# Batch 3's q and v loads and v casts moved, and batch 1's feature maps one slot earlier, in a fused attention and FFN kernel

## Chip, cores, metric

One NeuronCore of one Trainium2 chip. The metric is the time of one execution on the device in microseconds (us). The kernel was run several times; the profile is of one execution. Engines: PE is TensorE, DVE is VectorE, ACT is ScalarE, POOL is GpSimd, SP issues DMAs.

## The reference, cut to what matters

```python
def phi(x, c, s):                       # c, s: cos, sin of pi/2 * position / 576
    r = np.maximum(x, 0.0)
    return np.concatenate([r * c, r * s], axis=-1)
q_p, k_p = phi(q, cos_w, sin_w), phi(k, cos_w, sin_w)      # q, k, v: 8 batches, 8 heads, 576 x 64
kv  = np.einsum('bhsf,bhsd->bhfd', k_p, v)
z   = np.sum(k_p, axis=2)
num = np.einsum('bhsf,bhfd->bhsd', q_p, kv)
den = np.einsum('bhsf,bhf->bhs', q_p, z)[..., None] + 1e-06
# x = num / den, heads side by side: 4608 tokens x 512; then
xn  = x / np.sqrt(np.mean(x * x, axis=-1, keepdims=True) + 1e-06) * rms_g
g, val = xn @ w_gate, xn @ w_val        # 512 -> 1536
out = (silu(g) * val) @ w_out           # 1536 -> 512
```

## The kernel before

The program is scheduled by hand. Block b is the FFN of batch b (block 8 takes the last 64 tokens of every batch). A block has 16 slots: slots 0 to 11 make one 128-wide piece of gate and value each (8 matmuls on PE, 1.73 us, then `sg` = silu on ACT and the product `hT` on DVE), slots 12 to 15 make one output tile each (12 matmuls, 2.6 us). The attention of batch b+1 is strewn into block b: the helper `at(block, slot, where, f, ...)` puts a call before the slot's matmuls ("pe"), before its silu and product ("pre") or behind them ("post"). In the traces PE and DVE take their own lists in order (figures under step 3 below), so a slot number decides behind what an instruction stands. phi is the feature map of the reference, made of q and k in two halves (the cosine half on DVE, the sine half on ACT); `xnT` is x, normalised and transposed, which the FFN reads; the k-v product (`kv` and `z` of the reference) needs phi of k and v in bf16.

```python
# block 0: phi of k of batch 1, and q tile 0
for j in range(NJ):                                   # NJ = 9
    at(0, 7 + j // 2, "post", k_phi, V, 1, j, 0)      # cosine half on DVE
    at(0, 7 + j // 2, "post", k_phi, A, 1, j, 1)      # sine half on ACT
at(0, 11, "post", q_phi, V, 1, 0, 0)
at(0, 11, "post", q_phi, A, 1, 0, 1)
# ... (cut)
for nb in range(2, B):                                # batch nb is prepared in block b
    b = nb - 1
    late = nb == 2
    vb, vn = (b, 3) if late else (b - 1, 14)
    # ... phi of k at slots 12 to 14 of block b - 1 (cut)
    for c in range(5):                                # phi and DMA transpose of q, tile c
        qn = (2, 3, 5, 5, 6)[c] if late else c + 2 * (nb == 3)
        at(b, qn, "post", q_phi, V, nb, c, 0)
        at(b, qn, "post", q_phi, A, nb, c, 1)
        at(b, qn, "post", q_tr_dma, nb, c)
    if not late:
        at(vb, vn, "post", v_cast, V, nb, *LOW)       # v to bf16 on DVE, two halves
    at(vb, vn + 1, "post", v_cast, V, nb, *HIGH)
    kz, nds = (6, (7, 9, 11, 12)) if late else (4, (6, 8, 10, 12) if nb == 3 else (5, 7, 9, 11))
    at(b, kz, "pe", kvz_pe, nb, psA)                  # k-v product: 72 small matmuls, LOW then HIGH
    # ... its copies, the numerators nd at slots nds, x_norm and the xnT transpose a slot later (cut)
for nb in range(3, B):                                # loads, on SP
    b = nb - 2
    for i, which in enumerate(("k", "v", "q")):
        for p in range(5 if which == "q" else 4):     # 4 pieces of 256 or 288 KB; q also a tail
            n = (0, 6, 9)[i] + p if b == 1 else 5 * i + p
            at(b + n // 16, n % 16, "post", load_piece, which, nb, p)
# ... between blocks 0 and 1: output of block 0, attention of batch 1
for n in range(NNT - 2):
    if 1 <= n <= 4:
        q_tr_pe(1, n - 1, qbank[n - 1])               # PE transposes q of batch 1
    # ... (cut)
```

`raw` tiles of q and v exist once, so a load has to wait until the previous batch's phi or cast has read it. Block b+1 starts with matmuls on `xnT`, whose last quarter is a DMA transpose issued at slot 13 of block b.

Of the kernel before, what the change touches and what calls it, by code (L numbers as in the profile page):

```python
# [23 lines left out]
def kernel(  # L24
# [39 lines left out]
    V, A, G = nc.vector, nc.scalar, nc.gpsimd  # L64
    NJ = 9
    LOW, HIGH = (0, 2), (2, 4)
# [565 lines left out]
    def none():  # L632
        return {"pe": [], "mid": [], "pre": [], "post": []}
# [3 lines left out]
    def at(blk, n, where, f, *args):  # L637
        slots.setdefault((blk, n), none())[where].append((f, args))
# [17 lines left out]


    for j in range(NJ):
        at(0, 7 + j // 2, "post", k_phi, V, 1, j, 0)
        at(0, 7 + j // 2, "post", k_phi, A, 1, j, 1)  # L660
    at(0, 11, "post", q_phi, V, 1, 0, 0)
    at(0, 11, "post", q_phi, A, 1, 0, 1)


    for nb in range(2, B):
        b = nb - 1
        late = nb == 2
        vb, vn = (b, 3) if late else (b - 1, 14)
        if late:
            at(vb, vn, "post", v_cast, V, nb, *LOW)  # L670
        for j in range(NJ):
            kb, kn = (b, 1 + j // 7) if late else (b - 1, 12 + j // 3)
            if not late or j > 3:
                at(kb, kn, "post", k_phi, V, nb, j, 0)
            if not late or j > 1:
                at(kb, kn, "post", k_phi, A, nb, j, 1)
        for c in range(5):
            qn = (2, 3, 5, 5, 6)[c] if late else c + 2 * (nb == 3)
            at(b, qn, "post", q_phi, V, nb, c, 0)
            at(b, qn, "post", q_phi, A, nb, c, 1)  # L680
            at(b, qn, "post", q_tr_dma, nb, c)
        if not late:
            at(vb, vn, "post", v_cast, V, nb, *LOW)
        at(vb, vn + 1, "post", v_cast, V, nb, *HIGH)
        kz, nds = (6, (7, 9, 11, 12)) if late else (4, (6, 8, 10, 12) if nb == 3 else (5, 7, 9, 11))
        at(b, kz, "pe", kvz_pe, nb, psA)
        at(b, kz, "pre", kvz_evac, A, nb, psA, 0)
        at(b, kz, "pre", kvz_evac, A, nb, psA, 1)
        for j in range(4):
            n = nds[j]  # L690
            at(b, n, "mid" if n == NNT else "pe", nd_pe, nb, j, psA)
            at(b, n, "pre", nd_post, nb, j, psA)
            at(b, n, "post", x_sq, nb, j)
            where = "pre" if n + 1 >= NNT else "post"
            at(b, n + 1, where, x_norm, nb, j)
            at(b, n + 1, where, x_tr_dma, nb, j)
        if nb % 2 == 1:
            at(b, 13, "pe", nd_pe, nb, 4, psA)
            at(b, 13, "pre", nd_post, nb, 4, psA)
            at(b, 13, "post", x_sq, nb, 4)  # L700
            at(b, 14, "post", x_norm, nb, 4)
            at(b, 14, "post", x_tr_dma, nb, 4)
    for nb in range(3, B):

        b = nb - 2
        for i, which in enumerate(("k", "v", "q")):
            for p in range(5 if which == "q" else 4):
                n = (0, 6, 9)[i] + p if b == 1 else 5 * i + p
                at(b + n // 16, n % 16, "post", load_piece, which, nb, p)

    def gval_step(blk, n, bank=None):
# [31 lines left out]
    for n in range(NNT - 2):  # L743
# [4 lines left out]
        if 1 <= n <= 4:  # L748
            c = n - 1
# [22 lines left out]
        if n in nd_at:  # L772
            j = nd_at[n]
# [94 lines left out]
```

## Time and profile before

| | before |
|---|---|
| runs at hand for the prediction | 328.82, 559.21, 328.21 us |
| span of the profiled execution | 327.5 us, granted TensorE clock 1.00 |
| PE busy | 317.4 us (97%) |
| DVE, ACT busy | 57%, 54% |

The first line of the page's table of engines (busy time, share of the span, number of instructions):

```profile
PE 317.4 (97%) x2441; PEld 160.6 (49%) x2441; DVE 186.1 (57%) x412; ACT 176.6 (54%) x366; POOL 32.0 (10%) x67
```

With PE at 97%, only PE's idle time can be won. The list of waits, PE alone (total us, times, longest):

```profile
PE psO L479 <- ACT kpm L209: 1.7, 1, 1.7
PE psO L466 <- DVE warm L145: 1.2, 1, 1.2
PE psV L254 <- DVE qp L211: 1.0, 1, 1.0
PE psG L426 <- DMA xnT<-xn: 0.7, 1, 0.7
PE psG L565 <- DVE xnT L265: 0.5, 1, 0.5
PE psO L254 <- ACT qp L209: 0.3, 1, 0.3
```

All but the third and fourth lie in the first 20 us, which the change leaves alone. The third is here in the timeline (start, duration, engine, line, operation; in brackets the idle time before it and what ended it):

```profile
40.14 0.59 PE L446 MATMUL psC<-wo,hT 128*128 128x512 bf16 x2
40.37 2.55 ACT L209 ACTIVATE qp<-rq,tab 128x512 bf16<-128x512 f32 x4
40.41 0.69 DVE L441 TENSOR_TENSOR hT<-psV,sg 128x512 bf16<-128x512 f32 x1 [0.51 <-PE psV L426]
41.02 0.34 DVE L211 TENSOR_SCALAR kpm<-rk,tab 128x256 bf16<-128x256 f32 x1
41.28 1.12 DVE L211 TENSOR_SCALAR qp<-rq,tab 128x512 bf16<-128x512 f32 x2
...
42.16 0.33 PE L254 MATMUL psV<-ident,qp 128*128 128x128 bf16 x3 [0.99 <-DVE qp L211]
```

DVE started the product of slot 11 at 40.41, the last phi of k at 41.02 and phi of q at 41.28, in the order of its list, and PE waited 0.99 us for that. The fourth, in the timeline of the end of block 1, with the k-v product of batch 3 some 7 us later:

```profile
85.59 0.42 SPq L90 DMA_DIRECT2D rq<-in_q_dram  x1
...
87.02 1.70 SPq L406 DMA_TRANSPOSE xnT<-xn  x1
...
92.41 1.02 PE L426 MATMUL psG<-xnT,wg 128*128 128x512 bf16 x4 [0.73 <-DMA xnT<-xn]
...
99.41 1.34 PE L282 MATMUL psA<-vvm,kpm 64*128 64x65 bf16 x72
```

A piece of q goes out 1.43 us ahead of the transpose. The view of the tile `xnT`, cut to that transpose, gives the time from its issue to its landing:

```profile
L406 SPq DMA_TRANSPOSE xnT<-xn x1: 1698/1698/1698, 87.0 to 87.0; - x1
...
DMA to landing us min/median/max: 5.3/5.3/5.3
```

The k-v product runs through in 1.34 us; its v was cast in block 1.

### The profile page before, as it was taken

To read this page: it belongs to the slowest core of one execution; us is meant where nothing else is said; L and a number is where in the kernel's file an instruction comes from. 1 tells how busy PE (TensorE), PEld (TensorE's weight loads), DVE (VectorE), ACT (ScalarE), POOL (GpSimd) and SP (SyncE) were. 2 spreads that over 40 slices of the span, in tenths; PEclk is the share of its full clock that TensorE was granted. 3 is DMA by queue.
4 is the path that set the end of the run, shared out by engine and by line. 5 is a ranking of instruction groups with operands and counts; after the bars stand their busy time and mean duration, and the time that the engine had idled before them with its cause. 6 is when DMAs were issued, how large, how long until landed. Compare 5 with 4: busy or idle time off the path is not lost.

```text
span 327.5 us, 6440 instructions
## 1 busy us (share of the span) xinstructions
PE 317.4 (97%) x2441; PEld 160.6 (49%) x2441; DVE 186.1 (57%) x412; ACT 176.6 (54%) x366; POOL 32.0 (10%) x67
## 2 busy tenths in 40 slices
PE   6999989999999999999999999999999999999994
PEld 2587455554435444544454445444544444444442
DVE  6875668787745876578257745773577133203310
ACT  6963865965656457645654576556644233223321
POOL 1660022001100110011001100110011000000000
PEclk9999999999999999999999999999999999999999
DMA  7999999899978966976597569967621400020014
GB/s 253 244 195 266 309 174 331 311 170 220 235 202 154 228 171 169 218 208 164 179 221 195 150 197 214 188 174 214 127 47 32 130 32 0 29 101 1 0 34 96
DMA packets 80337, 53.91 MB, mean 165 GB/s; under 512 B 51377, under 2 KB 67761, under 8 KB 80306
## 3 DMA queue, kind: packets, MB, share of 16 engines
q1 hardware_dynamic: 73264, 48.64, 58.6%
q0 software_dynamic: 6880, 4.72, 10.1%
q8 instruction: 19, 0.31, 0.4%
q14 instruction: 12, 0.10, 0.2%
q10 hardware_dynamic: 162, 0.13, 0.1%
HBM read 37.75 MB, written 9.44 MB: 144 GB/s over the span
## 4 chain that ended last, share of the span: by engine, by line
PE 84%; ACT 5%; DVE 4%; DMA 3%; issue 2%; POOL 0%; ACTq 0%; DVEq 0%
PE psG L426 25%; PE psV L426 24%; PE psC L446 23%; PE psA L282 3%; ACT kpm L209 2%; PE psA L310 2%; DMA xnT<-xn 2%; PE psG L446 1%; PE psG L565 1%; DMA rk<-in_k_dram 1%; PE psV L565 1%; DVE xt L364 1%; PE psO L565 1%; DVE xn L387 1%; ACT sg L435 1%
## 5 line engine op out<-in xcount | busy, mean ns | idle before, releaser
L441 DVE TENSOR_TENSOR hT<-psV,sg 128x512 bf16<-128x512 f32 x102 | 70.3, 690 | 97.7 <-PE psV L426 86.8
L435 ACT ACTIVATE sg<-psG 128x512 f32<-128x512 f32 x102 | 60.6, 594 | 67.0 <-PE psG L426 66.9
L426 PE MATMUL psG<-xnT,wg 128*128 128x512 bf16 (+1 forms) x368 | 92.9, 375 | 0.8 <-DMA xnT<-xn 0.7
L426 PE MATMUL psV<-xnT,wv 128*128 128x512 bf16 (+1 forms) x368 | 92.7, 374 | 0.0
L446 PE MATMUL psC<-wo,hT 128*128 128x512 bf16 x396 | 89.6, 379 | 0.0
L426 PEld LDWEIGHTS <-wv 128*128 128x128 bf16 x416 | 40.6, 98 | 47.4
L446 PEld LDWEIGHTS <-hT 128*128 128x128 bf16 x420 | 40.2, 98 | 46.4
L426 PEld LDWEIGHTS <-wg 128*128 128x128 bf16 x416 | 38.5, 98 | 42.2 <-issue 1.0
L263 ACT COPY osb<-psC 128x512 f32<-128x512 f32 (+1 forms) x33 | 19.2, 582 | 41.0 <-PE psC L446 39.6
L380 POOL TENSOR_TENSOR rs<-ms,mhalf 128x1 f32<-128x1 f32 x36 | 19.8, 550 | 200.6 <-ACT scr L375 200.6
L387 DVE SCALAR_TENSOR_TENSOR xn<-xt,rs,gb 128x512 bf16<-128x512 f32 x36 | 26.8, 746 | 14.7 <-POOL rs L380 14.7
L375 ACT ACTIVATE scr<-xt 128x513 bf16<-128x513 f32 x36 | 22.9, 635 | 21.5 <-DVE xt L364 21.2
L209 ACT ACTIVATE kpm<-rk,tab 128x256 bf16<-128x256 f32 (+1 forms) x78 | 32.0, 477 | 1.7 <-DMA rk<-in_k_dram 1.7
L364 DVE TENSOR_TENSOR xt<-psA,rec 128x512 f32<-128x512 f32 x35 | 24.2, 691 | 1.2
L211 DVE TENSOR_SCALAR kpm<-rk,tab 128x256 bf16<-128x256 f32 (+1 forms) x84 | 22.3, 330 | 2.2 <-DMA rk<-in_k_dram 2.2
L209 ACT ACTIVATE qp<-rq,tab 128x512 bf16<-128x512 f32 x32 | 22.4, 713 | 0.0
L211 DVE TENSOR_SCALAR qp<-rq,tab 128x512 bf16<-128x512 f32 x32 | 15.3, 494 | 0.0
L310 PEld LDWEIGHTS <-qpT 128*128 128x128 bf16 x248 | 11.6, 98 | 6.7 <-issue 0.2
L310 PE MATMUL psA<-kvzs,qpT 128*128 128x65 bf16 x248 | 12.8, 194 | 0.2
L426 PE MATMUL psV<-xnt_tail,wv 128*128 128x512 bf16 x48 | 12.3, 379 | 0.0
L426 PE MATMUL psG<-xnt_tail,wg 128*128 128x512 bf16 x48 | 12.3, 379 | 0.0
L282 PEld LDWEIGHTS <-kpm 64*128 64x128 bf16 x576 | 9.9, 95 | 3.6 <-issue 3.1
(89 smaller groups left out, 166.7 us busy)
## 6 DMA issues: line engine op xcount, KB each, us to landing
out_dram<-osb SPq DMA_DIRECT2D x32, 256.0 KB, 2.5
rv<-in_v_dram SPq DMA_DIRECT2D x21, 288.0 KB, 3.4
rk<-in_k_dram SPq DMA_DIRECT2D x20, 288.0 KB, 3.6
rq<-in_q_dram SPq DMA_DIRECT2D x20, 256.0 KB, 3.4
rk<-in_k_dram SPq DMA_DIRECT2D x2, 1152.0 KB, 8.7
rq<-in_q_dram SPq DMA_DIRECT2D x2, 1024.0 KB, 8.9
rv<-in_v_dram SPq DMA_DIRECT2D x3, 576.0 KB, 8.6
wo<-in_moe_w_out_dram POOLq DMA_DIRECT2D x4, 384.0 KB, 7.1
```

The costliest lines, as they stand in the source:

```text
L209: nc.scalar.activation(out=out_ap, in_=in_ap, func=AF.Relu, scale=scale)
L211: eng.tensor_scalar(out=out_ap, in0=in_ap, scalar1=scale, scalar2=0.0, op0=ALU.mult, op1=ALU.max)
L282: nc.tensor.matmul(banks[c][:, r * E : (r + 1) * E], lhsT=kp_main[b][lo : lo + 64, j, r, :], rhs=vvm[b % 2][lo : lo + 64, r, j, :], start= ...
L310: nc.tensor.matmul(o[:, g, i, :], lhsT=qpT[(b, 0)][:, h, j * P : (j + 1) * P], rhs=kvz_of(b, h), start=True, stop=True,)
L364: nc.vector.tensor_tensor(out=xt[:, 0:DM].rearrange("p (b h d) -> p b h d", b=2, d=D), in0=o[:, :, :, 0:D], in1=rec[:, :, :].unsqueeze(3). ...
L375: nc.scalar.activation(out=scr[:, :], in_=xt[:, 0 : DM + 1], func=AF.Square, scale=1.0 / math.sqrt(DM), accum_out=ms[:, :],)
L380: nc.gpsimd.tensor_tensor(out=rs[:, :], in0=ms[:, :], in1=mhalf[:, :], op=ALU.pow)
L387: nc.vector.scalar_tensor_tensor(out=xn[:, :], in0=x_of[(b, j)][:, 0:DM], scalar=rs_of[(b, j)][:, :], in1=gb[:, :], op0=ALU.mult, op1=ALU. ...
L426: nc.tensor.matmul(pst[bank][:, cols[0] : cols[1]], lhsT=w[:, t, n * P : (n + 1) * P], rhs=x[:, t, cols[0] : cols[1]], start=(t == 0), sto ...
L435: nc.scalar.activation(out=sg[:, :], in_=psG[bank][:, :], func=AF.Silu)
L441: nc.vector.tensor_tensor(out=hTs[blk][:, n, :], in0=psV[bank][:, :], in1=sg[:, :], op=ALU.mult)
L446: nc.tensor.matmul(bank, lhsT=hTs[blk][:, n, j * P : (j + 1) * P], rhs=wo[:, n, :], start=(n == 0), stop=(n == NNT - 1),)
```

## The change

The intent, in the words that came with it: q of batch 3 loaded at slots 6 to 10 and v at 13 to 16 of block 1, v cast in block 2, phi of q as in later batches; for batch 1 the cosine half of q tile 0 a slot sooner (the diff moves phi of k a slot sooner too).

```diff
     for j in range(NJ):
-        at(0, 7 + j // 2, "post", k_phi, V, 1, j, 0)
-        at(0, 7 + j // 2, "post", k_phi, A, 1, j, 1)
-    at(0, 11, "post", q_phi, V, 1, 0, 0)
+        at(0, 6 + j // 2, "post", k_phi, V, 1, j, 0)
+        at(0, 6 + j // 2, "post", k_phi, A, 1, j, 1)
+    at(0, 10, "post", q_phi, V, 1, 0, 0)
     at(0, 11, "post", q_phi, A, 1, 0, 1)
@@
         vb, vn = (b, 3) if late else (b - 1, 14)
+        if nb == 3:
+            vb, vn = b, 1
@@
-            qn = (2, 3, 5, 5, 6)[c] if late else c + 2 * (nb == 3)
+            qn = (2, 3, 5, 5, 6)[c] if late else c
@@
-        at(vb, vn + 1, "post", v_cast, V, nb, *HIGH)
-        kz, nds = (6, (7, 9, 11, 12)) if late else (4, (6, 8, 10, 12) if nb == 3 else (5, 7, 9, 11))
+        at(vb, vn + 1 + (nb == 3), "post", v_cast, V, nb, *HIGH)
+        kz, nds = (6, (7, 9, 11, 12)) if late else (4, (5, 7, 9, 11))
@@
-                n = (0, 6, 9)[i] + p if b == 1 else 5 * i + p
+                n = (0, 13, 6)[i] + p if b == 1 else 5 * i + p
```

## The prediction

> **What bounds the kernel.** TensorE: the engine table has it busy 317.4 of 327.5 us, at granted clock 1.00; DVE 57%, ACT 54%. The list of waits puts most of PE's 10 us of idle time into the first 20 us, untouched by the change. Later, two exceed 0.3 us:
> - 0.99 us at 41.17-42.16: PE's transposes of q of batch 1 wait for phi of q tile 0 (cosine half on DVE from 41.28, behind hT of slot 11).
> - 0.73 us at 91.68-92.41: block 2 waits for the last xnT transpose, issued at 87.02, landing after 5.35 us (shortest: 2.6), beside pieces of q and output stores.
>
> **What the change does.** No work is added or removed. By the instruction order:
> 1. Block 0: phi of k of batch 1 goes from slots 7-11 to 6-10, and the cosine half of q tile 0 goes ahead of hT of slot 11. Its k landed at about 31.0 (issued 20.97, 10.0 us); ACT gets there at 31.4. Its q landed at about 39.7 (32.03 plus 7.6); DVE gets there at 39.65. Both just in time: the halves are done by 40.7, before PE asks at 41.0. The 0.99 us go; v's casts then bind perhaps 0.15. Gain 0.85 us.
> 2. Block 1: q's pieces move to slots 6-10, before the last transposes; v's come at 13-16, behind them. [...] I expect 2.8 to 4 us; there is room for 4.66. Gain 0.7 us.
> 3. Block 2: both casts of v leave the end of block 1 and stand on DVE at slots 1 and 3. The second comes after hT and phi of q of slot 3, while PE wants it in the k-v product right behind slot 3's matmuls; that product now waits for DVE twice, before not at all. With block 2 starting at 0, PE is there at 6.9 and through the first half at 7.55. DVE starts hT of slot 3 at 7.17 (0.69 us), then phi (0.48), the cast (0.75): done at 9.0. PE waits about 1.45 us, and nothing gives it back. Batch 2's product shows such a wait already (0.24 us, at 68.6). The last v piece is issued behind block 2's first q transpose (about 4.45, landing 3.6 us later: 8.05); late, it costs up to 1 us more.
> 4. phi of q and numerators of batch 3 come sooner: block 3 was not waiting, so nothing.
>
> **Sum.** -0.85 - 0.7 + 1.5 = about 0. Fast runs before: 328.2, 328.8. I predict 328.5 us, 327.2 to 330.0; chances 0.02 faster, 0.96 within 2%, 0.02 slower.
>
> **What would show it.** 1: no wait for DVE's qp near 41. 2: block 1's last xnT transpose lands in under 4.5 us and block 2 starts without a DMA wait. 3: a new wait of 1.3 to 2.5 us, PE's psA for DVE's vvm, some 7.5 us into block 2; the 72 small matmuls span 2.8 us instead of 1.34.
>
> **What would make it wrong.** q or k of batch 1 landing later (step 1 a loss of some tenths); v pieces slowing the transpose as q's did (step 2 nil); a late last v piece (step 3 to 2.5 us). Step 3 would be free only if DVE were ahead of PE, but hT of slot 3 can't start before slot 3's matmuls end.

One sentence of step 2, its reason why the transpose should land sooner, is cut, since no trace or run here shows it. The 2.8 to 4 us are for the landing of that transpose, the author's estimate between the 2.6 and 5.35 us that the profile of before shows. -0.85 - 0.7 + 1.5 comes to -0.05 us.

## The result, and the profile after

| | before | after |
|---|---|---|
| median | 328.84 us (6 runs, one of them 559.21, not a fast run and left out of the ratio) | 329.29 us (6 runs, 328.50 to 329.94) |
| ratio of fast runs | | 1.0015, 95% interval 0.9996 to 1.0033 |
| span of the profiled execution | 327.5 us | 327.7 us |

A ratio here is the mean time of one kernel's fast runs over that of the other's fast runs of the same rounds, so it is not quite the ratio of the medians. The change makes no difference that the runs can tell from nothing.

PE's list of waits after (line numbers are those of the changed file; the lines used here are the same):

```profile
PE psA L282 <- DVE vvm L265: 1.7, 1, 1.7
PE psO L479 <- ACT kpm L209: 1.3, 1, 1.3
PE psO L466 <- DVE warm L145: 1.2, 1, 1.2
PE psG L565 <- DVE xnT L265: 0.5, 1, 0.5
...
```

The waits for `qp` and for the `xnT` DMA are gone; one for `vvm` (the cast v) is new. The timeline at the end of block 0:

```profile
39.92 0.48 DVE L211 TENSOR_SCALAR qp<-rq,tab 128x512 bf16<-128x512 f32 x1
...
40.34 1.94 ACT L209 ACTIVATE qp<-rq,tab 128x512 bf16<-128x512 f32 x3
40.51 0.59 PE L446 MATMUL psC<-wo,hT 128*128 128x512 bf16 x2
40.78 0.69 DVE L441 TENSOR_TENSOR hT<-psV,sg 128x512 bf16<-128x512 f32 x1 [0.38 <-PE psV L426]
...
41.38 0.61 PE L254 MATMUL psV<-ident,qp 128*128 128x128 bf16 x8
```

DVE's half of q tile 0 now stands before the product of slot 11. PE transposes 0.87 us after its first output matmul, not 2.02 us. The end of block 1 and block 2 as far as the k-v product:

```profile
86.23 1.19 SPq L406 DMA_TRANSPOSE xnT<-xn  x1
...
88.08 0.43 SPq L79 DMA_DIRECT2D rv<-in_v_dram  x1
...
90.74 1.03 PE L426 MATMUL psG<-xnT,wg 128*128 128x512 bf16 x4
...
97.74 0.75 PE L282 MATMUL psA<-vvm,kpm 64*128 64x65 bf16 x36
97.91 0.69 DVE L441 TENSOR_TENSOR hT<-psV,sg 128x512 bf16<-128x512 f32 x1 [0.64 <-PE psV L426]
...
98.52 0.48 DVE L211 TENSOR_SCALAR qp<-rq,tab 128x512 bf16<-128x512 f32 x1
...
99.34 0.76 DVE L265 CAST vvm<-rv 128x1152 bf16<-128x1152 f32 x1 [0.34 <-DMA rv<-in_v_dram]
...
100.16 0.75 PE L282 MATMUL psA<-vvm,kpm 64*128 64x65 bf16 x36 [1.67 <-DVE vvm L265]
...
100.84 1.04 PE L426 MATMUL psG<-xnT,wg 128*128 128x512 bf16 x3
```

The product is cut in two halves of 36 matmuls with 1.67 us of nothing between them. What fills the gap is on DVE: product of slot 3, phi of q, 0.34 us of waiting for the last piece of v, the cast. The transpose of `xnT` has no load close ahead of it any more:

```profile
L406 SPq DMA_TRANSPOSE xnT<-xn x1: 1190/1190/1190, 86.2 to 86.2; - x1
...
DMA to landing us min/median/max: 2.4/2.4/2.4
```

To put sizes on this I cut PE's timeline at five starts of matmul groups, in every profile. A: up to the first output matmul of block 0. B: on to the first PE transpose of q of batch 1. C: on to the first matmul of block 2. D: on to the first gate matmul behind batch 3's k-v product. E: the rest. Times are us, differences of start times in the timeline; so they can hold more than the wait that the list shows. E is taken from a span that is printed to 0.1 us, so its second decimal means nothing.

| profile | A | B | C | D | E |
|---|---|---|---|---|---|
| before | 40.14 | 2.02 | 50.25 | 8.26 | 226.83 |
| after | 40.51 | 0.87 | 49.36 | 10.10 | 226.86 |
| difference | +0.37 | -1.15 | -0.89 | +1.84 | +0.03 |

B, C and D are the three parts of the change. They cancel to -0.20 us. A ends behind the moved phi of batch 1, but PE takes 10.36 us from its first matmul of slot 6 to the end of A in every profile here except e7 (10.77), so the spread of A comes from before that slot, which the change leaves alone.

### The profile page after: what moved, and what is told of

It reads as the page before. It is cut to its first block, busy times and chain, and to the rows that moved or that the text cites. A ratio compares the mean times of both kernels' runs of the same rounds, so it can differ in the third digit from the quotient of the medians.

```text
span 327.7 us, 6406 instructions
## 1 busy us (share of the span) xinstructions
PE 315.6 (96%) x2406; PEld 161.0 (49%) x2441; DVE 186.0 (57%) x412; ACT 176.7 (54%) x366; POOL 32.0 (10%) x67
## 3 DMA queue, kind: packets, MB, share of 16 engines
HBM read 37.75 MB, written 9.44 MB: 144 GB/s over the span
## 4 chain that ended last, share of the span: by engine, by line
PE 89%; DMA 4%; ACT 3%; DVE 2%; issue 1%; SPq 1%; ACTq 0%
PE psC L446 26%; PE psG L426 25%; PE psV L426 25%; DMA rv<-in_v_dram 4%; PE psA L282 3%; PE psA L310 2%; PE psG L446 1%; PE psG L565 1%; PE psV L565 1%; PE psO L565 1%; ACT sg L435 1%; ACT kpm L209 1%; PE psC L830 1%; PE psV L254 1%; ACT qp L209 1%
## 5 line engine op out<-in xcount | busy, mean ns | idle before, releaser
L426 PE MATMUL psG<-xnT,wg 128*128 128x512 bf16 (+1 forms) x352 | 90.9, 374 | 0.7
L446 PE MATMUL psC<-wo,hT 128*128 128x512 bf16 x382 | 88.2, 379 | 0.7
L282 PE MATMUL psA<-vvm,kpm 64*128 64x65 bf16 x540 | 10.6, 191 | 1.7 <-DVE vvm L265 1.7
```

What stands on the lines that cost most here:

```text
L282: nc.tensor.matmul(banks[c][:, r * E : (r + 1) * E], lhsT=kp_main[b][lo : lo + 64, j, r, :], rhs=vvm[b % 2][lo : lo + 64, r, j, :], start= ...
L426: nc.tensor.matmul(pst[bank][:, cols[0] : cols[1]], lhsT=w[:, t, n * P : (n + 1) * P], rhs=x[:, t, cols[0] : cols[1]], start=(t == 0), sto ...
L446: nc.tensor.matmul(bank, lhsT=hTs[blk][:, n, j * P : (j + 1) * P], rhs=wo[:, n, :], start=(n == 0), stop=(n == NNT - 1),)
```

## The experiments

The theory: three independent terms, as in the table. The main rivals were these: the gains only move a bound (what is won early is waited for at block 2); the new wait is due to v's landing and not to DVE's order; the wait at block 2 in the profile of before comes from something other than the piece of q, or is not always there.

Ratios are to the kernel before, run beside it. All outputs were correct.

| run | median us | ratio (95%) | A | B | C | D | E |
|---|---|---|---|---|---|---|---|
| before_again | 328.60, one run | | 40.52 | 1.76 | 49.36 | 8.27 | 226.89 |
| before_third | 328.35, one run | | 40.30 | 1.76 | 49.36 | 8.27 | 226.91 |
| before_fourth | 329.63, one run | | 41.17 | 2.03 | 49.52 | 8.27 | 226.91 |
| e1_batch1_only | 327.77 | 0.9969 (0.9949 to 0.9990) | 40.00 | 0.86 | 49.42 | 8.27 | 226.85 |
| e2_batch3_only | 331.49 | 1.0070 (1.0045 to 1.0096) | 41.54 | 1.77 | 49.35 | 10.24 | 226.80 |
| e3_kvz_slot5 | 327.78 | 0.9966 (0.9947 to 0.9985) | 40.60 | 0.87 | 49.36 | 9.99 | 225.18 |
| e3_again | 327.48 | 0.9966 (0.9950 to 0.9981) | 40.30 | 0.86 | 49.36 | 10.09 | 225.19 |
| e4_q_late | 328.90 | 1.0002 (0.9983 to 1.0021) | 41.84 | 1.89 | 49.36 | 8.26 | 226.85 |
| e5_qhalf_only | 327.57, one run | | 40.11 | 1.00 | 49.53 | 8.27 | 226.89 |
| e6_v_early | 330.73, one run | | 41.51 | 0.86 | 50.05 | 9.67 | 226.91 |
| e7_cast_slot2 | 328.48 | 0.9990 (0.9971 to 1.0008) | 41.23 | 0.86 | 49.74 | 8.27 | 226.90 |
| e8_batch1_qlate | 327.27 | 0.9965 (0.9948 to 0.9982) | 40.18 | 0.86 | 49.36 | 8.27 | 226.83 |

### e1: the batch 1 part alone

On the kernel before: `7 + j // 2` to `6 + j // 2` twice, and `at(0, 11, ... q_phi, V ...)` to `at(0, 10, ...)`.

> The kernel before with the batch 1 part of the change alone. My theory (three independent terms: batch 1 gains about 1.1 us from the end of block 0 to its first PE transpose, block 2's start gains 0.9, the k-v product of batch 3 loses 1.8): 1.0 us faster than before, ratio 0.9965 to 0.998; no PE wait for qp near 41, block 2 still waiting about 0.7 us for the DMA of xnT. Rival (the whole change only moves one bound: what is gained early is waited for later at block 2's start, because DMA sets that time): block 2 waits 1.5 us or more and the time equals before.

Measured: 0.9969, and B went to 0.86 as in the changed kernel. The rival falls, since the gain arrives in the time. But one expectation failed: block 2 was to wait about 0.7 us for `xnT`, with q's pieces where they had been, and it did not wait at all (C 49.42). That made the C term doubtful, and led to the repeats below.

### e2: the batch 3 part alone

On the changed kernel: the same three lines back as they were.

> The kernel after with the batch 1 part undone. My theory: the wait of about 1.0 us for qp near 41 is back, block 2 starts without a DMA wait, the k-v product of batch 3 waits 1.3 to 1.7 us for the cast of v: 0.9 us slower than before, ratio 1.002 to 1.004. Rival (the moved loads and the cast cost nothing net): ratio 0.997 to 0.999.

Measured: the waits came as expected:

```profile
PE psA L282 <- DVE vvm L265: 1.8, 1, 1.8
...
PE psV L254 <- DVE qp L211: 0.7, 1, 0.7
```

The time was 1.0070, well over the 1.002 to 1.004 expected. B to E add up to 288.16 us, against 286.67 for the mean of the four profiles of before (1.89, 49.62, 8.27, 226.89): +1.5 us, more than the +0.9 expected, because those four profiles put the C term at 0.26 and not 0.89, and D grew by 1.97 here, not 1.84. The rest lies in A, which is 1.0 us over the mean of before (40.53); its clock dips there, see e4. The record gives the mean granted clock of every timed run, and profiles with that dip have 0.993 to 0.995, all others 0.997 or more. Four of the six runs of e2 stand at 0.995 (331.5 to 332.3 us), but only two of the eleven of before (at 0.993). Sorted so after the fact, the runs at 0.997 or more give 330.24 us (two runs) against 328.70 (nine): +1.5 us, as B to E say.

### e3, twice: the k-v product of batch 3 one slot later

```diff
-        kz, nds = (6, (7, 9, 11, 12)) if late else (4, (5, 7, 9, 11))
+        kz, nds = (6, (7, 9, 11, 12)) if late else (5, (6, 8, 10, 12)) if nb == 3 else (4, (5, 7, 9, 11))
```

> The kernel after, but the k-v product of batch 3 one slot later (5) and its numerators at 6, 8, 10, 12, as before the change. My theory: the second cast of v is done about 9.35 us into block 2, the product's first half about then too, so the wait falls from 1.67 to at most 0.2 us, nothing else changes and it is 1.6 us faster than after, ratio to before 0.994 to 0.996. Rival (the wait only moves: the later numerators then delay block 3's xnT): a new wait of 1 us or more at the start of block 3 and a time within 0.3 us of after.

Measured: 0.9966. That is short of the 0.994 to 0.996 expected, which took the changed kernel to be as fast as the one before; against its 1.0015 it is the 1.6 us expected. The product runs through behind the cast, in the timeline:

```profile
99.19 0.77 DVE L265 CAST vvm<-rv 128x1152 bf16<-128x1152 f32 x1
...
99.56 1.33 PE L282 MATMUL psA<-vvm,kpm 64*128 64x65 bf16 x72
```

(In the table D is longer by the slot that now stands ahead of the product, and E shorter: D and E make 235.17, before 235.09, the same within the rounding of the span.) So the wait is all that the moved casts cost, and it was not passed on to block 3. The repeat, beside e8:

> The kernel after with the product of batch 3 at slot 5, once more, beside the run that keeps the casts in block 1. Theory: ratio 0.996 to 0.997 again and within 0.4 us of that run; the last xnT transpose lands in 2.4 to 2.9 us.

Measured: 0.9966 again, 0.2 us from e8's median; the transpose landed in 2.4 us.

### e4: only q's last piece and tail behind the transpose

On the kernel before, in the loop of the loads: `if b == 1 and which == "q" and p > 2: n = 11 + p`.

> The kernel before, with only the last piece of q of batch 3 and q's tail moved from slots 12 and 13 to 14 and 15 of block 1, behind the last transpose of xnT. My theory (the DMA piece issued 1.4 us ahead of that transpose slows it): it lands in 2.4 to 3.5 us in place of 5.35, block 2 starts without a DMA wait, 0.7 to 0.9 us faster than before, ratio 0.997 to 0.998. Rival (something else holds that transpose, such as the output stores): it still takes over 4.5 us and the time equals before.

Measured: no DMA wait (C 49.36; the trace has no landing for this transpose), but the time was 1.0002, not 0.997 to 0.998. Leaving out the runs at 0.995 or less, as under e2, does not bring it back (328.77 against 328.70 us). The gain that the first profile of before promised was not there to be had in most executions. This profile's own start was late, and the view by windows says with what (us; busy time of PE, PEld, DVE, ACT, POOL; granted TensorE clock; DMA share; GB/s):

```profile
5.00:10.00 5.00, 3.96 (x12) 0.95 (x10) 4.84 (x23) 5.00 (x17) 0.00 (x0) 0.94 1.06 357
10.00:15.00 5.00, 4.58 (x98) 3.84 (x98) 3.36 (x9) 3.27 (x9) 3.96 (x6) 0.71 0.97 179
```

The clock dipped to 0.71 in the third stretch of 5 us. The same dip, 0.71 to 0.74, is in e2 and e6 and in no other of the 14 profiles; their A of 41.5 to 41.8 are the three longest (the others: 40.0 to 41.2). The same view, asked for two finer stretches, shows it whole:

```profile
6.03:9.44 3.41, 2.38 (x8) 0.52 (x6) 3.25 (x17) 3.41 (x13) 0.00 (x0) 1.00 1.06 366
9.45:12.85 3.40, 3.40 (x43) 2.49 (x44) 3.15 (x7) 2.33 (x4) 1.81 (x3) 0.50 0.82 218
```

The clock stood at 0.50 for some 3.4 us, which by this view is 1.7 us of full clock lost; in e2 and e6 it did so for as long, from 9.44 and 9.17 us. The A of the three are 1.0 to 1.3 us over the mean of the four profiles of before (40.53). How busy PE was just before does not tell these profiles from others: 2.38 of the 3.41 us ahead of the dip (e2: 2.67, e6: 2.59), and 2.31 us from 5.35 to 8.76 in before_third, which did not dip. What does go with the dip is a time: in the clock records of the traces the first one at full clock starts at 5.75 to 6.03 us in these three profiles, and at 3.95 to 5.35 or 6.26 to 7.02 us in the other eleven. No run here varied it, and the cause of the dip stays open.

### before, three more profiles

Nothing edited.

> The kernel before once more, unchanged, to see whether the DMA wait at block 2's start is there in every execution: the run with only the batch 1 part lost it too, its last transpose of xnT landing in 4.5 us with q's pieces where they were. If q's pieces make it wait always: 5 us or more to landing and a wait of 0.6 to 0.9 us. If 4.66 us of room is met in most executions and missed by jitter in some: 4.0 to 4.6 us to landing and no wait.

> The kernel before, a third profile. With the same loads ahead of it the last xnT transpose of block 1 took 5.3, 3.7, 4.5 and 2.7 us to land in four profiles so far (two of before, two with block 1's loads unchanged); only the first made PE wait. Theory (contention with q's piece widens and lengthens the landing, but 4.66 us of room is mostly enough): between 2.6 and 5.5 us, no wait more likely than not. Rival (the wait is the rule and the others were lucky): 4.8 us or more and a wait.

> The kernel before, a fourth profile; as for the third. If three of four show no wait, the gain of the moved loads is to be put at a quarter of the 0.7 to 0.9 us that the first profile showed.

Measured, landing of the last `xnT` transpose in before_again, before_third and before_fourth, in this order:

```profile
L406 SPq DMA_TRANSPOSE xnT<-xn x1: 1389/1389/1389, 87.2 to 87.2; - x1
...
DMA to landing us min/median/max: 3.7/3.7/3.7
```

```profile
L406 SPq DMA_TRANSPOSE xnT<-xn x1: 1202/1202/1202, 86.9 to 86.9; - x1
...
DMA to landing us min/median/max: 4.2/4.2/4.2
```

```profile
L406 SPq DMA_TRANSPOSE xnT<-xn x1: 1202/1202/1202, 88.1 to 88.1; - x1
...
DMA to landing us min/median/max: 4.6/4.6/4.6
```

PE had 4.66 us of room. The 3.7 us of before_again lie below both ranges that were expected; the other two fit the theory's range, though that contention is the reason no run shows. With a piece of q issued some 1.4 us ahead, six profiles (four of before, e1, e5) give 5.3, 3.7, 4.2, 4.6, 4.5 and 2.7 us; only the first shows a wait in the list, and the 4.6 us of before_fourth made block 2 start 0.17 us late. With a piece of v ahead instead (e6, e7) it is 5.1 and 4.7. Without one (after, e2, e3 twice) it is 2.4, four times; e8, like e4, has no landing in its trace and no wait. An output store goes out 1.6 to 2.0 us ahead of the transpose in every profile (2.0 in before as in after), so the store alone is not the reason. So at this place the load ahead of it goes with a slow and uneven transpose, and e6, which moves v's loads alone, brings that back; but block 2 mostly did not pay. Over the four profiles of before, C averages 49.62, so 0.26 us over 49.36, in place of the 0.89 of the first.

A load ahead is not enough by itself, though. Later than 100 us the 14 profiles hold 46 transposes of `xnT` with a piece of q issued 1.3 to 1.5 us ahead, and all of them landed in 2.4 to 2.8 us; the 2.6 us that the prediction names as the shortest had a piece of q 1.6 us ahead too. The view by windows has the DMA engines moving 243 GB/s at 84 to 88 us of before, and 153 to 155 GB/s in the like stretches around three of the later transposes (149.5, 182.9 and 216.8 us on, 4 us each). That what is in flight already is what counts would be a guess; no run here varies that apart from the place of the piece, and it stays open.

### e5: only DVE's half of q tile 0

On the kernel before: only `at(0, 11, ... q_phi, V, 1, 0, 0)` to slot 10; phi of k stays.

> The kernel before with only the cosine half of q tile 0 of batch 1 a slot sooner, phi of k left at slots 7 to 11. Theory (DVE's order is what held PE near 41; ACT's half was done 41.08, about when PE asked at 41.0): first PE transpose 0.9 to 1.0 us after the end of block 0, in place of 2.02, nearly all of the gain. Rival (moving phi of k is needed): 1.4 us or more.

Measured: B 1.00, and no wait of PE for `qp`. That is nearly the whole gain, so DVE's order held PE up. B alone flatters it, though: the k-v product of batch 1 then comes 0.16 us later (that is in its C), which moving phi of k as well avoids.

### e6: v's loads two slots earlier

On the changed kernel: `n = (0, 13, 6)[i] + p` to `(0, 11, 6)[i] + p`.

> The kernel after with the four v pieces two slots earlier, at 11 to 14 of block 1, casts left at slots 1 and 3. Theory (of the 1.67 us wait in the k-v product, 0.34 is the last v piece landing late and the rest DVE's order): no DMA wait of the cast, PE waits 1.3 to 1.4 us, product spans 2.75. Rival (landing of v is the cause): the wait is under 0.5 us. For the transpose at block 1's end: with a v piece issued about 1.4 us ahead of it, as q's was, it should land in 3.8 to 4.6 us in place of 2.4 to 2.9.

Measured, in the timeline:

```profile
99.42 0.75 PE L282 MATMUL psA<-vvm,kpm 64*128 64x65 bf16 x36
...
100.60 0.76 DVE L265 CAST vvm<-rv 128x1152 bf16<-128x1152 f32 x1
101.41 0.75 PE L282 MATMUL psA<-vvm,kpm 64*128 64x65 bf16 x36 [1.23 <-DVE vvm L265]
```

The cast no longer waits for its data, and PE still waits 1.23 us (1.3 to 1.4 expected): so of the 1.67, about 0.44 came from the last piece of v landing late and 1.23 from DVE's order. The rival (v's landing) falls. With v's piece ahead of it the transpose took 5.1 us (3.8 to 4.6 expected), and block 2 waited 0.5 us for it.

### e7: v's loads earlier and the second cast at slot 2

e6, and `vn + 1 + (nb == 3)` back to `vn + 1`.

> The kernel after with v's pieces at slots 11 to 14 of block 1 and the second cast at slot 2 of block 2 in place of 3. Theory (the cast must end before slot 3's matmuls do): DVE ends it about 7.4 us into block 2, before the first half of the product is through at 7.55, so no wait of PE for vvm; as fast as the run with the product at slot 5, ratio to before 0.995 to 0.998. Rival (DVE has no room and falls behind): a new wait of 0.5 us or more in slots 3 to 5.

Measured: the product runs through (D 8.27), and DVE keeps up:

```profile
96.56 0.76 DVE L265 CAST vvm<-rv 128x1152 bf16<-128x1152 f32 x1
...
98.28 0.76 DVE L265 CAST vvm<-rv 128x1152 bf16<-128x1152 f32 x1
...
98.83 1.34 PE L282 MATMUL psA<-vvm,kpm 64*128 64x65 bf16 x72
```

The theory of the order is confirmed: put the cast behind slot 2's work and the wait is gone. The time, 0.9990, is less good than the 0.995 to 0.998 expected. Its C is 0.38 us over 49.36, of which 0.2 are at block 2's start (v's piece ahead of the transpose) and 0.16 between the products of batches 1 and 2; and its A is late by 0.7 us, without a dip of the clock: 0.41 of it arises from slot 6 of block 0 on, where PE waits 0.24 us for a piece of the value weights, the rest before. Whether these hold in all its executions was not looked into.

### e8: the batch 1 part, q late, the casts where they were

e1 and e4 together.

> The kernel before with the batch 1 part of the change and with q's last piece and tail at slots 14 and 15 of block 1, all casts of v where they were. Theory: no wait for qp, none at block 2's start, none in the k-v product: 1.0 to 1.3 us faster than before, ratio 0.996 to 0.997, the same as the run with the product at slot 5. Rival (moving v's casts out of block 1's end is worth something by itself): the run with the product at slot 5 is faster by 0.4 us or more.

Measured: 0.9965, B 0.86, C 49.36, D 8.27. It ties with e3, so moving v's casts out of the end of block 1 is worth nothing by itself.

e1, e3 and e8 are faster than before by 0.3%, with intervals below 1. All three keep the batch 1 part and have no wait in batch 3's k-v product. The changed kernel stands at 1.0015 to the same kernel before, so e3 and e8 beat it by about 0.5% (0.9966 or 0.9965 over 1.0015; they were not run in the same rounds).

## Why the prediction was right or wrong

The number held: 328.5 us predicted with 327.2 to 330.0, 329.29 measured; no difference beyond 2%, and terms that cancel. Point by point:

- **What bounds the kernel: right.** E, 69% of the span, is 226.8 to 226.9 us in every profile whose k-v product stayed at slot 4. Only waits of PE, and the start (A), moved the time.
- **Step 1 (batch 1): right.** Predicted gain 0.85 us. B fell from 1.89 (mean of four profiles of before) to 0.87, so 1.02; 1.15 against the first profile. e1 shows it in the time and e5 that DVE's order is the reason. The 0.15 us that v's casts should take back did not show in the changed kernel (C has the same 49.36 as two profiles of before), only in e5.
- **Step 2 (the transpose): direction right, size wrong, mechanism not shown.** The step as put: "I expect 2.8 to 4 us; there is room for 4.66. Gain 0.7 us." The transpose did get faster, 2.4 us. But 0.7 was read from one execution, whose landing of 5.3 us was the worst of six; on average of four profiles the gain is 0.26 us. e1 and e4 pointed to it, the repeats showed it. What the runs show at this place is 2.4 us without and 2.7 to 5.3 us with a load ahead; that the landing is so uneven with one was the thing to know. Nor is a load ahead the whole of it, as the 46 later transposes show.
- **Step 3 (the cast behind phi of q): right.** Predicted 1.45 us, up to 1 more if v is late, with DVE free at 8.25 us into block 2 (its cast done at 9.0, less 0.75) and v landed at 8.05. In the profile DVE was free at 8.26 (98.52 + 0.48 - 90.74), v was there at 8.60, PE waited 1.67. The piece was issued at 4.76, not 4.45. D grew by 1.84, since the product spans 3.17 us in two halves (97.74 to 100.91) and 1.34 in one; e6 parts it into order (D +1.41) and landing (the other 0.43). This rests on PE and DVE taking their instructions in order, and the traces agree. PE was idle for 1.67 us while matmuls of slot 4 stood ready behind the product: the `psG` that they write had been read by 95.85, their `xnT` was in use from 90.74 on, and they started at 100.84. DVE ran the second cast at 98.28 in e7, where it stands behind slot 2's work, and at 100.60 in e6, with the same loads of v, where it stands behind slot 3's, neither time waiting for data.
- **Step 4 (earlier numerators): right.** No wait at block 3, in any profile.
- **Sum.** With the averages, -1.02 - 0.26 + 1.83 is +0.55 us, or +0.17% of 328.8; the runs gave +0.15% with an interval that holds zero. The prediction's sum was -0.05: step 2 gave 0.44 us less, step 3 took 0.33 more, step 1 gave 0.17 more. Every one of these lies well within 2%, and the predicted range is 2.8 us wide, so the number would have held had step 2 or step 3 come to nothing; it is the waits, not the number, that bear the steps out.

The level of single runs, the miss of e2 and part of the miss of e7 come from the start, A, which varies by 1.8 us between profiles of programs that PE runs alike up to there. The dip of the clock goes with the three longest; for the rest of A's spread I have no cause.

## What to carry to other kernels

When work is moved to take pressure off a place, look at what now stands right ahead of its consumer on the engine that makes it: a cast moved behind slot 3's work on DVE cost PE 1.8 us although DVE was 57% busy, and one slot of distance either way removed it (the product later in e3; the cast, with its loads, earlier in e7). Split a change whose sum is nought: here one third gained 1.0 us, one third lost 1.8, and each was worth keeping or mending by itself. A short DMA wait in one profile is one draw from a spread (here 5.3, 3.7, 4.2 and 4.6 us to landing in four profiles of one kernel); profile the unchanged kernel a few times before pricing it.
